# Two plain pairs instead of three before Strassen's algorithm in the output projection, and PSUM banks dealt round-robin over three tiles

## The chip, the cores and the metric

The kernel runs on one core of a Trainium2 chip. The metric is the device time of one execution in microseconds (us); the median of the runs counts.

## What is computed

Four sequences of 448 tokens pass through a talking-heads attention with 12 heads of 64 columns. The result, 1792 tokens by 768 columns, is the input `x` of this layer:

```python
h = x @ w_in                                  # 1792 x 1024
sm = softmax(h); solu = h * sm
ln = (solu - mean) / sqrt(var + 1e-6) * g_ln
out = ln @ w_out                              # 1792 x 768, float32
```

The change concerns only the last product, `ln @ w_out`, with 1024 rows and 768 columns in `w_out`.

## The kernel before, in words

Tokens go in 14 tiles of 128 (`NT = 14`). Each tile's 1024 hidden columns are made by 36 matmuls of 512 columns (`hidden`, L984) in one of three PSUM tiles `h_banks` of two banks each, `h_banks[t % 3]`. VectorE, ScalarE and GpSimd turn them into the SoLU and the layer norm (L1559 to L1659), as a high and a low fp16 half, `lh` and `ll`. Both halves are stored to DRAM (`zS`, L1662) and read back transposed into `lt` by a DMA on SyncE's queue (`zT`, `turn`, L1674).

The output projection handles tiles in seven pairs (`NPP = 7`). Each operand is split in a high and a low half, and each product sums three terms (high by high, high by low, low by high), all matmuls with 384 output columns (`project`, L1751). The first `NPL` pairs are **plain**: four products (two tiles by two halves of the columns), each over all eight blocks of 128 rows of `w_out`, so 24 matmuls each and 96 for the pair. They go in turn to the PSUM tiles of `ps_x` and `ps_y`, one bank each. The other pairs go by **Strassen's algorithm** (in Winograd's form) over the 2 by 2 blocks of the pair of tiles and `w_out`: seven products of 12 matmuls, 84 for the pair. For these a pair needs a **front**: two sums of the halves of `lt` into `xs` (`pair_whole`, L1689), four sums of blocks (`pair_sum`, L1702), two casts on ScalarE (`part_hi`, L1707) and two differences (`part_lo`, recorded at L1511). The emission of a Strassen product (`emit`) is one copy on ScalarE (product 0, L1772) or one or two VectorE operations (L1783), nine in all; that of a plain product is one scaled copy on either engine (L1762, L1764).

`w_out` too needs sums of its blocks, made in place from `wo_raw`, block row by block row k = 0 to 3: scaling (`zs`, L1506), four subtractions on VectorE (`zt`, L1511, into `tt` and `wo`), casts on ScalarE (L1541) and differences on VectorE (`zL`, L1511). The last of them overwrites the right half of the upper half of `wo_h` and `wo_l`, and so follows the first two products of the last plain pair (`zP`, `NPL - 1`).

The order of the work on each engine comes from a planner, `moe.order()`: it simulates the engines, takes for each the task that can start first, and among tasks that can start within 0.143 us the one with the earliest due time. The engines then run their instructions in that order, each waiting for what it needs. The due times of the projection follow `T = TP + TQ * (7 * i + min(i, NPL))`, 1.94 us per 12 matmuls: a pair's front is due 18 to 12 us before the pair, its emissions 12 us before the end of their product, so long overdue when they can run. The sums of `w_out` are due at fixed times (120 + 4 k).

Memory also hangs on `NPL`. `lt` of a pair lies in one of two `lt` buffers, except for the pairs `NPL` and `NPL + 1`, which take over `xf1` and `xf2`, the buffers of the inputs of batches 1 and 2. `xs` of pair `NPL` takes over `xf0`; the later ones take turns in the two `raw` buffers, which are free once `wo_raw` has been used up:

```python
n = i - NPL + 1
if 0 < n < B - 1:
    x = wt_p.tile(x_in[n].shape, F16, tag=f"xf{n}", name=f"lt_{i}")
```

The six Strassen banks are the two banks of each of the three tiles `h_banks`; `bank(i, j)` says which product takes which. The planner counts six banks (`B=6`). The semaphores come from the tile framework.

Of the kernel before, what the change touches and what calls it, by code (L numbers as in the profile page):

```python
# [240 lines left out]
def kernel(  # L241
# [82 lines left out]
    def spread_steps(out, am, n, name, bank):  # L324


        ps = []

        def turn():
            ps.append(bank(f"spread_{name}"))  # L330
            for i in range(n):
                nc.tensor.matmul(
                    ps[0][:, i * 128 : (i + 1) * 128],
                    am[:, i : i + 1].to_broadcast([128, 128]),
                    ident32,
                    start=True,
                    stop=True,
                )

        def take():  # L340
            x = ps[0][:, 0 : n * 128].rearrange("p (n f) -> p n f", n=n)
            nc.vector.tensor_reduce(out=out, in_=x, axis=AX.X, op=ALU.max)

        return [("pe", turn), ("dve", take)]

    def scale_steps(am, n, e, name, bank, pool=const):

        t = pool.tile([128, 2], F32, name=f"amx_{name}")
        own, am1 = t[:, 0:1], t[:, 1:2]
        s, inv, steps = pow2_steps(am1, 1, e, name, pool)  # L350

        def join():
            nc.vector.tensor_reduce(out=own, in_=am, axis=AX.X, op=ALU.max, apply_absolute_value=True)

        steps = [("dve", f) for f in steps]
        return s, inv, [("dve", join)] + spread_steps(am1, own, 1, name, bank) + steps
# [600 lines left out]
    NT = NTOK // 128  # L957
# [3 lines left out]
    h_banks, hps = [], {}  # L961
# [439 lines left out]
    with tc.manual_schedule():  # L1401
# [91 lines left out]
            nc.vector.tensor_scalar(out=c_out, in0=i_o, scalar1=2.0**-E_LN, scalar2=None, op0=ALU.mult)  # L1493

        KH, DH, FH = KFF // 2, DM // 2, DFF // 2
        NPP, NPL = NT // 2, 3
        STEPS = [(i, j) for i in range(NPP) for j in range(4 if i < NPL else 7)]
        tz, tts = {}, {}

# [232 lines left out]

        def bank(i, j):
            n = (7 * (i - NPL) + j) % 6
            return h_banks[n // 2][:, n % 2, 0:DH]

        def project(i, j):
            if i < NPL:
# [334 lines left out]
```

## Time and profile before

| | us |
|---|---|
| median of 3 runs (646.65 to 649.11) | 648.18 |
| the profiled execution itself | 645.8 |
| its span, first to last instruction | 644.1 |
| TensorE busy in the span | 619.3 |
| VectorE busy in the span | 542.9 |

The profiled execution takes 1.7 us beyond its span, and lies 2.4 us under the median of the runs. In the rows below times are from the start of the span. A row of the timeline says when it begins, how long it lasts, engine, line, operation, out<-in, and in square brackets the idle time of the engine before it with what ended it. PE is TensorE, DVE VectorE, ACT ScalarE, POOL GpSimd, SPq and ACTq the queues of SyncE and ScalarE.

### The profile page before, as it was taken

To read this page: it belongs to the slowest core of one execution; us is meant where nothing else is said; L and a number is where in the kernel's file an instruction comes from. 1 tells how busy PE (TensorE), PEld (TensorE's weight loads), DVE (VectorE), ACT (ScalarE), POOL (GpSimd) and SP (SyncE) were. 2 spreads that over 40 slices of the span, in tenths; PEclk is the share of its full clock that TensorE was granted. 3 is DMA by queue.
4 is the path that set the end of the run, shared out by engine and by line. 5 is a ranking of instruction groups with operands and counts; after the bars stand their busy time and mean duration, and the time that the engine had idled before them with its cause. 6 is when DMAs were issued, how large, how long until landed. Compare 5 with 4: busy or idle time off the path is not lost.

```text
span 644.1 us, 17785 instructions
## 1 busy us (share of the span) xinstructions
PE 619.3 (96%) x6612; PEld 425.6 (66%) x6612; DVE 542.9 (84%) x1361; ACT 471.3 (73%) x1046; POOL 280.3 (44%) x427
## 2 busy tenths in 40 slices
PE   7889989999999999999999999999999999999995
PEld 7557767777767778777877777774444445566663
DVE  7879997789988689996999989848999698877873
ACT  5788978999888898988989997726766688432120
POOL 2125773255844254594354246403688656400000
PEclk9999999999999999999999999999999999999998
DMA  9057488466678448779746763019993111896122
GB/s 257 3 194 233 152 171 179 156 201 211 207 170 181 149 137 241 239 167 235 239 145 229 218 209 122 3 35 340 263 270 83 67 65 50 202 213 142 50 82 66
DMA packets 118063, 105.88 MB, mean 164 GB/s; under 512 B 70052, under 2 KB 105176, under 8 KB 117976
## 3 DMA queue, kind: packets, MB, share of 16 engines
q1 hardware_dynamic: 110456, 86.88, 47.6%
q0 software_dynamic: 4416, 12.40, 7.1%
q10 hardware_dynamic: 3104, 5.46, 2.7%
q8 instruction: 52, 0.85, 0.6%
q14 instruction: 35, 0.29, 0.1%
HBM read 33.24 MB, written 16.97 MB: 78 GB/s over the span
## 4 chain that ended last, share of the span: by engine, by line
PE 62%; DVE 19%; ACT 7%; issue 4%; POOL 3%; DMA 3%; SPq 1%; DVEq 0%; ACTq 0%; POOLq 0%
PE po L766 15%; PE ps_h L984 13%; PE ps_h L1751 8%; PE px L815 7%; PE pm L711 6%; PE ps L644 6%; PE y L1751 5%; DVE dead L721 4%; DVE s L661 3%; ACT e L737 3%; DMA sr<-s 2%; ACT s L656 2%; DVE hl_k L365 2%; POOL wr L758 1%; DVE wo_l L365 1%
## 5 line engine op out<-in xcount | busy, mean ns | idle before, releaser
L766 PE MATMUL po<-wr,e 128*112 128x120 f32 x1440 | 175.0, 272 | 6.4 <-POOL wr L758 4.9
L766 PEld LDWEIGHTS po<-wr,e 128*112 128x112 f32 x1440 | 155.7, 177 | 36.6 <-POOL wr L758 15.9
L758 POOL TENSOR_SCALAR wr<-wq,sm 128x120 f32<-128x120 f32 x180 | 77.3, 437 | 180.5 <-DVE sm L752 93.4
L737 ACT ACTIVATE e<-pm,nb,c_exp 128x448 f32<-128x448 f32 x180 | 131.5, 735 | 18.6 <-DVE dead L721 9.4
L721 DVE TENSOR_SCALAR_CACHE_REDUCE dead<-pm,c_nexp 128x448 f16<-128x448 f32 x180 | 121.7, 676 | 11.5 <-PE pm L711 7.5
L661 DVE SCALAR_TENSOR_TENSOR s<-ps,s 120x448 f16<-120x448 f32 (+1 forms) x192 | 112.2, 615 | 14.4 <-ACT s L656 13.9
L369 ACT COPY p_t<-po 112x480 f32<-112x480 f32 x180 | 108.2, 625 | 11.1 <-PE po L766 9.8
L656 ACT ACTIVATE s<-ps 120x448 f16<-120x448 f32 (+1 forms) x192 | 97.5, 554 | 16.4 <-PE ps L644 15.8
L815 PE MATMUL px<-p_t,raw_v 112*64 112x120 f32 (+3 forms) x1632 | 86.8, 259 | 0.8 <-ACT e L737 0.7
L815 PEld LDWEIGHTS px<-p_t,raw_v 112*64 112x64 f32 x1632 | 76.1, 137 | 16.1 <-issue 11.0
L984 PE MATMUL ps_h<-wi,xf 128*128 128x512 f16 x396 | 85.8, 379 | 0.0
L644 PE MATMUL ps<-k,q 64*64 64x448 f16 (+2 forms) x1008 | 78.5, 354 | 3.1 <-DVE s L661 2.3
L984 PEld LDWEIGHTS <-xf 128*128 128x128 f16 x396 | 38.7, 98 | 46.5
L1751 PEld LDWEIGHTS <-lt 128*128 128x128 f16 x432 | 42.3, 98 | 28.9 <-issue 1.0
L711 PE MATMUL pm<-sr,wp_hi 64*64 64x448 f16 x720 | 56.4, 359 | 2.1 <-DMA sr<-s 1.1
L644 PEld LDWEIGHTS <-q 64*64 64x64 f16 (+2 forms) x1008 | 34.5, 106 | 24.6 <-issue 8.3
L1751 PE MATMUL y<-wo_h,lt 128*128 128x384 f16 x192 | 47.2, 326 | 0.6 <-DVE o L1764 0.6
L1659 POOL TENSOR_TENSOR ll<-u,lh 128x1024 f16<-128x1024 f32 x14 | 33.3, 2379 | 11.4 <-ACT lh L1655 11.4
L737 ACT ACTIVATION_READ_ACCUMULATOR e<-pm,nb,c_exp 128x1 f32 x180 | 37.8, 210 | 0.0
L711 PE MATMUL pm<-sr,wp_lo 64*64 64x448 f16 (+1 forms) x360 | 36.1, 349 | 0.0
L365 DVE SCALAR_TENSOR_TENSOR xsl<-px,x_sc,xsh 128x120 f16<-128x120 f32 (+1 forms) x96 | 25.9, 325 | 7.9 <-ACT xsh L360 7.9
L748 DVE TENSOR_SCALAR sm<-sm 128x2 f32<-128x2 f32 (+1 forms) x92 | 18.8, 204 | 15.1 <-ACT e L737 14.4
(209 smaller groups left out, 950.4 us busy)
## 6 DMA issues: line engine op xcount, KB each, us to landing
sr<-s SPq DMA_DIRECT2D x176, 210.0 KB
cv_wi<-in_moe_w_in_dram SPq DMA_DIRECT2D x24, 256.0 KB
cv_wo<-in_moe_w_out_dram SPq DMA_DIRECT2D x8, 768.0 KB
raw_k<-in_k_dram POOLq DMA_DIRECT2D x18, 224.0 KB, 3.6
raw_q<-in_q_dram POOLq DMA_DIRECT2D x18, 224.0 KB, 5.0
raw_v<-in_v_dram POOLq DMA_DIRECT2D x18, 224.0 KB, 3.9
ln_h<-lh SPq DMA_DIRECT2D x14, 256.0 KB
ln_l<-ll SPq DMA_DIRECT2D x14, 256.0 KB
```

The source lines that it names most:

```text
L369: nc.scalar.copy(out=out, in_=in_)
L644: nc.tensor.matmul(sps[b, c, h + e][lo:hi], q2[b, g][rows, 2 * j + x, i0 + lo : i0 + hi], k1[b, g][rows, 2 * j + y], start=(a == 0), stop= ...
L656: nc.scalar.activation(out=s_t[b, c][0 : y.shape[0], h, 0], in_=y, func=AF.Copy, scale=2.0**-E_S)
L661: nc.vector.scalar_tensor_tensor(out=t[:, h, 1], in0=y, scalar=2.0**-E_S, in1=t[:, h, 0], op0=ALU.mult, op1=ALU.subtract)
L711: nc.tensor.matmul(pmx[b, u + i][64 * e : 64 * e + 64, 0:S], w[rows], sr[b, u][rows, e, z], start=(a == 0), stop=(a == 2),)
L721: nc.vector.tensor_scalar(out=dead, in0=pmx[b, u][:, 0:S], scalar1=c_nexp[0:UK, b : b + 1], scalar2=None, op0=ALU.mult, op1=ALU.min, accum ...
L737: nc.scalar.activation(out=ee[b, u], in_=pmx.pop((b, u))[:, 0:S], func=AF.Exp, bias=nbs.pop((b, u)), scale=c_exp[0:UK, b : b + 1], accum_o ...
L758: ENG[eng].tensor_scalar(out=w, in0=wq[0:UK, 0 : H * UN], scalar1=sm, scalar2=1.0, op0=ALU.mult, op1=ALU.mult)
L766: nc.tensor.matmul(ps[:, c * 120 : (c + 1) * 120], e[:, c * CP : (c + 1) * CP], w, start=True, stop=True)
L815: nc.tensor.matmul(xps[b, blk, g][e * 64 : e * 64 + 64, i, cut], raws["v", b, p][:, e, c * D : (c + 1) * D], next(x for y, x in block_view ...
L984: nc.tensor.matmul(ps[:, n], xx[:, kc, o : o + 128], ww[:, kc, n * 512 : (n + 1) * 512], start=(kc == 0 and a == 0), stop=(kc == KDM - 1 a ...
L1751: nc.tensor.matmul(y, x, w, start=(n == 0), stop=(n == len(terms) - 1 ))
```

## The change

Two plain pairs are left of three, so that pairs 2 to 6 go by Strassen's algorithm. Product n (counted through all Strassen pairs) takes bank n div 3 of tile n mod 3 in place of bank n mod 2 of tile n div 2 (n taken mod 6).

```diff
         KH, DH, FH = KFF // 2, DM // 2, DFF // 2
-        NPP, NPL = NT // 2, 3
+        NPP, NPL = NT // 2, 2
         STEPS = [(i, j) for i in range(NPP) for j in range(4 if i < NPL else 7)]
         tz, tts = {}, {}
...
         def bank(i, j):
             n = (7 * (i - NPL) + j) % 6
-            return h_banks[n // 2][:, n % 2, 0:DH]
+            return h_banks[n % 3][:, n // 3, 0:DH]
```

## Rows read from the trace of the kernel before

**Rows 1.** The page: busy us of the engines, share of the span, instructions.
```profile
PE 619.3 (96%) x6612; PEld 425.6 (66%) x6612; DVE 542.9 (84%) x1361; ACT 471.3 (73%) x1046; POOL 280.3 (44%) x427
```
**Rows 2.** Chain that ended last, by time: start, us, engine, tile, line, count.
```profile
432.30 79.17 PE ps_h L984 x366
...
551.18 31.45 PE y L1751 x192
582.63 54.61 PE ps_h L1751 x336
```
**Rows 3.** Windows, whole projection: us, then busy (count) PE, PEld, DVE, ACT, POOL, PEclk, DMA.
```profile
534.84:637.30 102.46, 101.81 (x625) 60.95 (x623) 77.62 (x113) 33.93 (x57) 16.04 (x10) 1.00 0.52 121
```
**Rows 4.** Waits of TensorE, 430 to 644 us: total, times, longest.
```profile
PE y L1751 <- DVE o L1764: 0.6, 1, 0.6
```
**Rows 5.** Groups of instructions, 540 to 644.1 us: busy, mean ns, idle before.
```profile
L1702 DVE TENSOR_TENSOR xs<-xs 128x512 f32<-128x512 f32 x16 | 11.0, 688 | 0.4
...
L1511 DVE TENSOR_TENSOR sz<-xs,sz 128x1024 f16<-128x1024 f32 x8 | 9.7, 1217 | 0.4 <-ACT sz L1707 0.4
L1783 DVE SCALAR_TENSOR_TENSOR o<-ps_h,c_out,xs 128x384 f32<-128x384 f32 x16 | 9.6, 612 | 4.6 <-PE ps_h L1751 4.6
L1689 DVE TENSOR_TENSOR xs<-lt 128x1024 f32<-128x1024 f16 x8 | 9.6, 1218 | 0.0
```
**Rows 6.** Timeline of the first Strassen pair, at the boundaries of its products.
```profile
584.41 0.33 PE L1751 MATMUL ps_h<-tz_h,lt 128*128 128x384 f16 x1
...
586.37 0.33 PE L1751 MATMUL ps_h<-wo_h,lt 128*128 128x384 f16 x1
...
586.57 0.58 ACT L1772 ACTIVATE xs<-ps_h,c_out 128x384 f32<-128x384 f32 x1 [3.32 <-PE ps_h L1751]
...
590.47 0.62 DVE L1783 SCALAR_TENSOR_TENSOR o<-ps_h,c_out,xs 128x384 f32<-128x384 f32 x1 [0.93 <-PE ps_h L1751]
...
597.22 0.61 DVE L1783 SCALAR_TENSOR_TENSOR o<-ps_h,c_out,xs 128x384 f32<-128x384 f32 x1
```
**Rows 7.** Timeline of VectorE at the end, after the last matmul.
```profile
637.27 0.62 DVE L1783 SCALAR_TENSOR_TENSOR o<-ps_h,c_out,o 128x384 f32<-128x384 f32 x1 [1.58 <-PE ps_h L1751]
637.80 1.13 DVE L1783 SCALAR_TENSOR_TENSOR o<-ps_h,c_out,xs 128x384 f32<-128x384 f32 x2
```
**Rows 8.** Windows, two stretches of stores (columns as in rows 3; last is GB/s).
```profile
630.50:632.60 2.10, 2.10 (x15) 1.26 (x14) 0.18 (x1) 0.00 (x0) 0.00 (x0) 1.00 0.33 94
638.90:642.20 3.30, 0.00 (x0) 0.00 (x0) 0.04 (x1) 0.00 (x0) 0.00 (x0) 0.74 0.69 178
```
**Rows 9.** Windows, before and in the plain pairs (columns as in rows 3).
```profile
505.00:512.00 7.00, 7.00 (x35) 3.38 (x34) 2.71 (x10) 4.50 (x10) 2.89 (x3) 1.00 0.29 112
512.00:527.00 15.00, 15.00 (x71) 6.82 (x70) 14.33 (x26) 12.42 (x20) 8.01 (x5) 1.00 0.14 53
527.00:543.00 16.00, 16.00 (x89) 8.43 (x87) 13.04 (x30) 13.13 (x29) 7.10 (x7) 1.00 0.13 51
543.00:551.00 8.00, 7.60 (x47) 4.47 (x46) 7.86 (x7) 4.34 (x8) 7.51 (x5) 1.00 0.30 118
551.00:567.00 16.00, 15.82 (x97) 9.48 (x97) 12.91 (x20) 8.88 (x14) 4.19 (x2) 1.00 0.97 212
```
**Rows 10.** Timeline of VectorE: sums of w_out, an emission, w_out's last difference.
```profile
545.43 2.30 DVE L1511 TENSOR_TENSOR tt<-wo,tt 128x384 f32<-128x384 f32 x1
547.77 2.36 DVE L1511 TENSOR_TENSOR wo<-wo,tt 128x384 f32<-128x384 f32 x1
550.05 0.55 DVE L1511 TENSOR_TENSOR wo<-wo,wo 128x384 f32<-128x384 f32 x1
550.52 0.60 DVE L1764 TENSOR_SCALAR o<-y,c_out 128x384 f32<-128x384 f32 x1
...
565.23 0.55 DVE L1511 TENSOR_TENSOR tz_l<-wo,tz_h 128x384 f16<-128x384 f32 x1
```
**Rows 11.** Windows, the second Strassen pair (columns as in rows 3).
```profile
596.10:609.80 13.70, 13.70 (x87) 8.25 (x85) 11.75 (x17) 2.67 (x3) 0.00 (x0) 1.00 0.21 59
```

## The prediction

> **What bounds the kernel now.** I read the page first: TensorE is busy for 619.3 of 644.1 us of the span [rows 1]. The chain that ended last shows where this binds. From 432.3 us on it names long runs of TensorE, and its last two, 31.45 and 54.61 us, are the projection up to 637.24 us [rows 2]; what lies between the runs is work behind TensorE, since the windows show it busy for 101.81 of 102.46 us of the projection at the full granted clock, 2.4 GHz [rows 3]. Third, its waits: one, of 0.6 us, for a VectorE emission [rows 4]. So in this stage a matmul saved is time saved, until VectorE comes too late. After the last matmul 6.9 us of the span are left (644.1 - 637.24). The sum is made against the profiled execution's own 645.8 us (span 644.1 and 1.7 around it) and carried to the median, 648.18 us, 2.4 us above it.
>
> **Matmuls removed.** Pair 2 needs 84 matmuls in place of 96. 336 take 54.61 us, 0.1625 us each [rows 2], so 12 x 0.1625 = **-1.95 us**, all on the path. Bounds: 12 x 0.164 from the plain run (31.45 / 192) and 12 x 0.1625: one answer.
>
> **Banks.** An emission is late in a regular way. Product 0 of the first Strassen pair ends near 584.4, where product 1 begins; its emission waits until 586.57, just after product 1 ended at 586.4 [rows 6]. Product 2 ends at 588.3, its emission starts at 590.47, at the end of product 3 [rows 6]. Both times the two products share a PSUM tile, in different banks: the wait is for the tile. Afterwards the next product lies in another tile, and an emission can begin as its own product ends. In mid-stage this gains nothing, as TensorE doesn't wait. At the end it does. The last pair has product 5 in the first bank of a tile and product 6 in its second, so product 5's two operations run only after product 6, at 637.27 and the first half of 637.80, ahead of product 6's own, which ends at 638.93 [rows 7]. Afterwards product 5 is emitted during product 6, and product 6's one operation runs at 637.27 and ends at 637.89: **-1.04 us**. The stores follow. Now a whole tile and half of one, 178 GB/s x 3.3 us = 587 KB, go out together and end near 642.1, 3.2 us after the last emission; half a tile alone, 94 x 2.1 = 197 KB, was out 1.9 us after its emission ended at 630.7 [rows 8]. Afterwards the whole tile's emission ends 1.13 us behind product 5 (637.24 - 1.95 + 1.13 = 636.4), 1.5 us ahead of the half's: up to **-1.3 us** more. Bounds -1.04 (the stores still collide) and -2.34 (they don't); I take **-2.0**, nearer the second, since 393 KB at 178 GB/s need 2.2 us and overlap the half's store for 0.7 us only.
>
> **The front of one more pair.** 2 x 1.218 + 4 x 0.688 + 2 x 1.217 = **7.6 us of VectorE** [rows 5], and two casts on ScalarE, which is busy 8.88 of 16 us there [rows 9] and covers them. Emissions: nine operations of 0.61 [rows 5] and one on ScalarE in place of four, some 3 us more, but late, where VectorE has 1.95 us free in a pair's 13.7 us with a front included [rows 11]. The 7.6 us come early: the Strassen pairs now begin 96 matmuls, 15.6 us, sooner, at about 567 us, and front 2 must be done 3 products later. Its due time lies ahead of those of w_out's sums, so the planner puts it before them. Its input is no obstacle: `lt` of pair 2 moves into `xf1`, free when the last tile of batch 1 has been multiplied, four hidden tiles of 36 x 0.2163 = 7.8 us before 534.84, so at 503.7 [rows 2, 3]. These four transposes move from behind plain pair 0 to there, on SyncE's queue ahead of layer-norm stores; what those feed is transposed 20 us later or more, so I cost it at nothing (uncovered it would be 4 issues).
>
> Where does front 2 fit? VectorE is idle for 4.29 us from 505 to 512, of which at most half comes after the transposes have landed; for 0.67 to 527, 2.96 to 543, and 0.14 to 551 [rows 9]: at best 5.9 us. The rest, and idle time that sits inside dependent chains, pushes the queue. Behind it on VectorE stand the sums of w_out and, in order, the emission of plain pair 0's third product. Before, that emission ran at 550.52 and already held TensorE for the 0.6 us of rows 4; all matmuls of pair 1 queue behind it. Why it is late shows above it: two of w_out's subtractions of 384 columns took 2.30 and 2.36 us, the next 0.55 [rows 10], while GpSimd was busy 7.51 of 8 us [rows 9]. The Trainium skill (page "SBUF — State Buffer", section "Who interferes with whom") says that a VectorE instruction with two SBUF inputs and a GpSimd instruction that reads SBUF exclude each other for a whole instruction. The trace agrees with that, and the rule speaks against this change, whose eight new VectorE operations all have two SBUF inputs and fall beside the layer norm.
>
> The cost has no row of its own. From below: -0.6 us, if the planner's new order puts the emission earlier. From above: 7.6 us of work and half of the eight operations stretched by 1.8 us (2.36 - 0.55), 14.8 us, less 5.9 of idle time: 8.9 us. I take **+2.1 us** of new stall at plain pair 1: 7.6 less the 3.8 us idle from 512 to 551 leaves 3.8, and of w_out's sums ahead of the emission (4 x 0.55 = 2.2) some will be planned behind it. It is nearer to the lower end because TensorE, once held, gives every later user that much slack: the stalls do not add, the largest counts.
>
> **Later.** w_out's last difference ended at 565.8 us [rows 10], with 3.1 us of VectorE idle in the last 16 [rows 9]; their use begins after about 568.7, so a delay of 3 us is covered, the more so after the stall. Front 3 can start only when `wo_raw` is free, near 571, and is needed at about 586: 7.6 us and seven products' emissions, 5.5, fit into 15.
>
> **The new wait.** If a tile is the unit, product n+3 now waits for emission n (before: n+6 for n and n+1). From the end of product n to the start of n+3 there are two products, 3.9 us. Product 5 of the first pair ended at 584.41 + 5 x 1.95 = 594.2 and its emission at 597.83 [rows 6]: 3.6 us, with two of the old waits before it. I cost it at nothing; if the cover goes, some tenths each time, and everything on TensorE queues behind.
>
> **Sum.** -1.95 - 2.0 + 2.1 = -1.85 us: from 645.8 to 643.95 for the profiled execution, **646.3 us** for the median.
>
> **Rivals.**
> First: no new stall. For it: planned early, front 2 has up to 5.9 us of gaps, and w_out's sums may be planned behind the emission. Against: rows 4 and 10 show the emission late already. Time 648.18 - 3.95 = 644.2; 643.6 if the old 0.6 goes too.
> Second, slower: VectorE is the bound at plain pair 1. Every second operation of front 2 is held by GpSimd, the stall is 8.9 us, the time 648.18 - 3.95 + 8.9 = 653.1. For it: rows 10; against: of 39 us before 551 only the last 8 have GpSimd at 94%, the others at about half [rows 9]. The time is above that of before from 4.0 us of stall. By the page's rule just cited this is what must happen if the front is planned into those last 8 us.
> Third: product n+3 waits for emission n. At 0.7 us once in each of five pairs, 3.5 us, without the forecast's stall: 647.7. For: 3.6 of 3.9 us used. Against: that lateness is mostly the wait that the change takes away.
> Fourth, the change does not do what it says: the emissions wait for something other than the tile, the tail stays, and with my stall 648.3 comes out. Rows 6 and 7 speak against it.
>
> **Chances.** Forecast 0.40, first 0.32, second 0.12, third 0.10, fourth 0.06. About 0.5%, 3.2 us, can be told from no change here. Faster by more (under 644.9): the first and a little of the forecast, 0.34. Slower by more (over 651.4): most of the second, 0.10. Same: 0.56. The range takes in the first with the old stall gone and the tail's lower bound (648.18 - 1.95 - 2.34 - 0.6 = 643.3), the third and fourth, and the second up to half of its stall beyond the forecast's: 643.0 to 650.5.
>
> **What would show it.** Right: 612 matmuls in the projection; the first emission of a pair begins at the end of its own product; after the last matmul one VectorE operation, and 4.6 to 5.9 us of span left; TensorE's waits with one of 2 to 3.5 us for the emission of plain pair 0, behind two-input operations at 1.4 us or more. Wrong: no such wait (then the first), waits for Strassen emissions in each pair (third), several us of waits for `tz` or `sz` (front or sums late), or a tail of 6.9 us.

## The result: 7.6 us faster, more than the range allowed

The changed kernel took a median of 640.68 us (639.51 to 641.25, 5 runs) against 648.26 us (646.65 to 649.11, 5 runs) of the kernel before in the same comparison: ratio 0.9896, interval 0.9866 to 0.9926. The forecast was 646.3 us, with a range of 643.0 to 650.5. The same kernel compared again (below) gave 0.9936 (0.9914 to 0.9958). A ratio of 0.992 lies in both intervals, and it is what the profiles show: the output projection with its tail (the time from the last matmul to the end of the span) is **5.1 us** shorter.

### The profile page after: what moved, and what is told of

Its sections match the earlier page's. It is cut to its first block, busy times and chain, and to the rows that moved or that the text cites. A ratio compares the mean times of both kernels' runs of the same rounds, so it can differ in the third digit from the quotient of the medians.

```text
span 637.8 us, 17788 instructions
## 1 busy us (share of the span) xinstructions
PE 617.1 (97%) x6600; PEld 424.3 (67%) x6600; DVE 552.5 (87%) x1378; ACT 473.2 (74%) x1045; POOL 285.0 (45%) x427
## 3 DMA queue, kind: packets, MB, share of 16 engines
q10 hardware_dynamic: 2720, 4.42, 2.3%
## 4 chain that ended last, share of the span: by engine, by line
PE 69%; DVE 14%; ACT 7%; issue 3%; POOL 3%; DMA 2%; SPq 0%; DVEq 0%; ACTq 0%; POOLq 0%
PE ps_h L984 17%; PE po L766 15%; PE ps_h L1751 11%; PE px L815 8%; PE ps L644 6%; PE pm L711 6%; PE y L1751 5%; DVE dead L721 3%; DVE s L661 3%; ACT e L737 3%; ACT s L656 2%; DVE hl_k L365 2%; POOL wr L758 1%; DMA raw_q<-in_q_dram 1%; ACT p_t L369 1%
## 5 line engine op out<-in xcount | busy, mean ns | idle before, releaser
L656 ACT ACTIVATE s<-ps 120x448 f16<-120x448 f32 (+1 forms) x192 | 97.6, 555 | 16.2 <-PE ps L644 15.6
L1751 PEld LDWEIGHTS <-lt 128*128 128x128 f16 x372 | 36.4, 98 | 24.2
L1659 POOL TENSOR_TENSOR ll<-u,lh 128x1024 f16<-128x1024 f32 x14 | 31.9, 2276 | 11.4 <-ACT lh L1655 11.2
L1751 PEld LDWEIGHTS <-sz 128*128 128x128 f16 x240 | 23.5, 98 | 15.5
```

What stands on the lines that cost most here:

```text
L656: nc.scalar.activation(out=s_t[b, c][0 : y.shape[0], h, 0], in_=y, func=AF.Copy, scale=2.0**-E_S)
L1751: nc.tensor.matmul(y, x, w, start=(n == 0), stop=(n == len(terms) - 1 ))
```

## The profile after

The profiled execution took 639.51 us, its span is 637.8. First the page's busy times, against [rows 1]:

```profile
PE 617.1 (97%) x6600; PEld 424.3 (67%) x6600; DVE 552.5 (87%) x1378; ACT 473.2 (74%) x1045; POOL 285.0 (45%) x427
```

TensorE works 2.2 us less and VectorE 9.6 us more. The chain that ended last, against [rows 2]:

```profile
431.04 79.17 PE ps_h L984 x366
...
510.43 23.38 PE ps_h L984 x108
533.81 31.20 PE y L1751 x192
565.01 68.26 PE ps_h L1751 x420
```

From 431 us up to the last matmul the chain is TensorE alone, and the list of TensorE's waits is empty from 420 us to the end: the 0.6 us of [rows 4] are gone. 612 matmuls end at 633.27, and the span ends 4.53 us later, where it was 6.86. The windows, against [rows 3] and [rows 9]:

```profile
512.00:527.00 15.00, 15.00 (x71) 6.75 (x70) 14.90 (x24) 13.39 (x22) 7.13 (x5) 1.00 0.10 37
527.00:543.00 16.00, 16.00 (x90) 8.66 (x89) 15.64 (x29) 14.33 (x27) 11.70 (x8) 1.00 0.63 119
543.00:551.00 8.00, 8.00 (x51) 4.81 (x50) 7.90 (x13) 6.38 (x13) 3.99 (x3) 1.00 0.44 159
551.00:567.00 16.00, 16.00 (x101) 9.63 (x99) 15.59 (x25) 8.34 (x15) 5.80 (x4) 1.00 0.79 180
567.00:583.00 16.00, 16.00 (x100) 9.65 (x99) 15.76 (x23) 3.26 (x4) 0.00 (x0) 1.00 0.58 134
533.81:633.30 99.49, 99.45 (x613) 59.69 (x610) 87.19 (x131) 34.36 (x54) 18.75 (x11) 1.00 0.49 114
```

The fourth number is VectorE's. From 512 to 583 us it is idle for 1.2 us in 71: the front of the additional pair has filled every gap, and still TensorE (the second number) waits for nothing. Where the emission that was expected to be late stands, shows VectorE's timeline:

```profile
542.57 2.46 DVE L1511 TENSOR_TENSOR tt<-wo,tt 128x384 f32<-128x384 f32 x1
...
545.98 1.28 DVE L1587 SCALAR_TENSOR_TENSOR u<-ps_h,sm,u 128x1024 f32<-128x1024 f32 x1
...
547.18 0.61 DVE L1764 TENSOR_SCALAR o<-y,c_out 128x384 f32<-128x384 f32 x1
...
549.52 0.55 DVE L1511 TENSOR_TENSOR tt<-wo 128x384 f32<-128x384 f32 x1
550.11 2.37 DVE L1511 TENSOR_TENSOR tt<-wo,tt 128x384 f32<-128x384 f32 x1
```

L1764 is the emission of plain pair 0's third product. It begins at 547.18, at 550.52 before [rows 10], although more work lies before it in all: the sums of `w_out`'s block row 1 (from 549.52 on) now come behind it. The end, against [rows 7]:

```profile
631.35 0.62 DVE L1783 SCALAR_TENSOR_TENSOR o<-ps_h,c_out,o 128x384 f32<-128x384 f32 x1 [0.68 <-PE ps_h L1751]
...
632.52 1.74 SPq L2035 DMA_DIRECT2D out_dram<-o  x2
632.52 1.80 ACTq L2035 DMA_DIRECT2D out_dram<-o  x2
...
633.30 0.62 DVE L1783 SCALAR_TENSOR_TENSOR o<-ps_h,c_out,xs 128x384 f32<-128x384 f32 x1 [0.81 <-PE ps_h L1751]
```

Product 5 ends at 633.27 - 1.95 = 631.32 and is emitted at once; its stores leave at 632.52, and only one operation is left after the last matmul.

## The experiments

The question is what the gain is made of and why no stall came. Medians scatter by some us, but one stretch hardly does, so every profile was read in the same way: the **projection** runs from the first matmul of L1751 in the timeline to the end of the last one in the chain, the **tail** from there to the end of the span.

| kernel | projection | tail | sum | ratio to before (interval) |
|---|---|---|---|---|
| before | 102.40 | 6.86 | 109.26 | |
| before, again | 102.40 | 6.85 | 109.25 | 0.9999 (0.9981 to 1.0016) |
| emission first | 101.57 | 6.92 | 108.49 | 0.9991 (0.9971 to 1.0010) |
| banks alone | 102.38 | 4.45 | 106.83 | 0.9977 (0.9955 to 0.9998) |
| pairs alone | 99.61 | 6.01 | 105.62 | 0.9950 (0.9927 to 0.9972) |
| the change | 99.62 | 4.53 | 104.15 | 0.9896 (0.9866 to 0.9926) |
| the change, again | 99.62 | 4.41 | 104.03 | 0.9936 (0.9914 to 0.9958) |
| sums first | 101.26 | 4.46 | 105.72 | 0.9941 (0.9917 to 0.9965) |
| front twice | 99.62 | 4.44 | 104.06 | 0.9963 (0.9940 to 0.9986) |
| late sum | 102.92 | 4.42 | 107.34 | 0.9957 (0.9936 to 0.9978) |
| two PSUM tiles | 99.69 | 4.43 | 104.12 | 0.9916 (0.9889 to 0.9942) |
| late store | 99.63 | 4.65 | 104.28 | 0.9954 (0.9921 to 0.9986) |
| store behind | 99.62 | 5.84 | 105.46 | 0.9924 (0.9898 to 0.9950) |
| one plain pair | 113.30 | 4.50 | 117.80 | 1.0136 (1.0107 to 1.0165) |

("Pairs alone": there the chain does not pass through the last product, so the end is taken from the timeline, whose last matmul begins at 633.66 and takes 0.33 us: 633.99.)

### Both kernels once more, no edit

> The kernel before, unchanged, against itself. Both theories: ratio 1.000, within 0.2%. It gives the scatter: theory one (the stage before the projection only scatters) expects the projection to begin anywhere from 533.5 to 536 us in profiles of one and the same kernel; theory two (the change also makes the attention faster, by 1 to 2 us) expects 534.8 within 0.3 us, as in the profile before.

> The change as it is. Theory one: 5.3 us of the difference lie in the projection and its tail (1.95 matmuls, 1.0 stalls of TensorE, 2.3 behind the last matmul), the rest is scatter, so the difference comes out nearer to 5.3 than to 7.6 us and the projection begins at a scattered time. Theory two: 7 us or more again, and the projection begins 1 us or more sooner than in the null run.

The kernel before repeats itself: 0.9999, and its projection begins at 535.05 us, which fits both theories. The change is again faster, but by 4.5 us in the medians (642.57 against 647.06), not 7.6, and its projection begins later, at 541.97: theory one. Its profiled run took 647.76 us, though projection and tail are as short as in the first. The time is lost before, which the chain shows:

```profile
306.72 6.30 DMA cv_wi<-in_moe_w_in_dram
...
313.04 10.89 DMA cv_wi<-in_moe_w_in_dram
...
438.37 71.41 PE ps_h L984 x330
...
511.14 3.21 DMA lt<-ln_l
...
514.42 3.13 DVE xs L1689
...
524.48 3.08 DVE xs L1689
...
532.86 1.30 DVE u L1587 x2
534.20 7.93 PE ps_h L984 x36
```

Two things. The long run of hidden matmuls begins at 438.37, at 431.04 in the first profile, after loads of `w_in` that don't stand in the first chain; up to there the order of TensorE's instructions is the same in both kernels. In 14 profiles it begins between 431.04 and 438.37, so that the attention alone scatters by 7 us, and the first profile is the earliest of all. And the run now breaks off after 330 matmuls: the last hidden tile waited 0.9 us, and the chain leads back over both L1689 operations of the new front to the transposes. That wait comes with the change, and the forecast had it nowhere (why it is 0 in one profile and 0.9 in the other: last section).

### One half of the change at a time

```diff
-        NPP, NPL = NT // 2, 3
+        NPP, NPL = NT // 2, 2
```

> Two plain pairs, banks as before. Theory that the banks give the tail: 12 matmuls (1.95 us) and the old stall go (1.0 us), the tail behind the last matmul stays at 6.9 us: 3 us faster than before. Rival: with one more Strassen pair the products are counted from another start, the last pair's product 5 takes bank 33 mod 6 = 3 (second of the middle tile) and product 6 bank 34 mod 6 = 4 (first of the last tile), so they lie in different tiles with the old dealing too: the tail is 4.5 us and the whole gain of 5.3 us is there without the new banks.

```diff
-            return h_banks[n // 2][:, n % 2, 0:DH]
+            return h_banks[n % 3][:, n // 3, 0:DH]
```

> Three plain pairs, banks dealt over the tiles. Theory: 624 matmuls, the stall of 0.6 us at the second plain pair stays, emissions of the first product of a pair begin at the end of their own product, the tail goes from 6.9 to 4.5 us: 2.3 us faster than before, and TensorE waits for no Strassen emission. Rival (product n+3 waits for emission n too often): waits of TensorE for VectorE or ScalarE in each Strassen pair, 2 to 4 us in all, and no gain.

The banks alone give -2.43 us, all in the tail, and leave the 0.6 us wait as it was. The pairs alone take 2.79 us off the projection: 1.95 of matmuls and 0.8 for the wait, which is gone. They also give 0.85 of the tail, which is between the theory (nothing) and the rival (all of it), since counting from pair 2 puts the last two products into different tiles:

```profile
632.08 0.62 DVE L1783 SCALAR_TENSOR_TENSOR o<-ps_h,c_out,xs 128x384 f32<-128x384 f32 x1 [2.10 <-PE ps_h L1751]
...
633.79 1.13 DVE L1783 SCALAR_TENSOR_TENSOR o<-ps_h,c_out,xs 128x384 f32<-128x384 f32 x2
```

Here product 4 waits for its mate 5 (until 632.08), so four operations of products 4 and 5 stand ahead of product 6's, which ends at 634.92, 0.93 us after the last matmul. So the halves overlap by about 1 us: -2.43 - 3.64 would be -6.1, and the whole gives -5.1.

### Why the old stall went: the planner's order

On the kernel before, the sums of block row 1 were put behind the emission; on the changed kernel, the emission behind these sums.

```diff
 # emission first, on the kernel before: the task zt of w_out's sums
+                    behind=[("zE", 0, 2)] if (k, i) == (1, 0) else [],
 # sums first, on the changed kernel: the task zE
-                behind=[("zE",) + x for x in before],
+                behind=[("zE",) + x for x in before] + ([("zt", 1, 3)] if (i, j) == (0, 2) else []),
```

> The kernel before, but the planner must put the sums of w_out's block row 1 behind plain pair 0's third emission. Theory (the order alone made the old stall): TensorE's wait of 0.6 us goes and the projection and its tail take 108.3 us in place of 109.3. Rival (the old stall came from GpSimd slowing VectorE, whatever the order): the wait stays at 0.5 us or more.

> The change, but the planner must put plain pair 0's third emission behind the four sums of w_out's block row 1, as it stood in the kernel before. Theory (the forecast stall was right in its mechanism and did not come because the planner put the emission ahead of these sums): the emission, at 547.2 us in the changed kernel, now follows operations that end there at 554 us, so TensorE waits 3 to 5 us at the second plain pair and the projection and its tail take 107 to 109 us in place of 104.0. Rival (VectorE has slack there whatever the order): a wait under 1 us, 104 to 105 us.

The order is enough to remove the stall. With the emission first the kernel before has no wait, and its projection is 0.83 us shorter, at 101.57; the change then has exactly 101.57 - 1.95 = 99.62. (In the kernel before the sums ahead of the emission were also stretched [rows 10]; no run takes the stretch away and leaves the order, so what each is worth alone stays open.) The run with the sums first did not reach its order on the engines: the planner put the emission later, but gave it to ScalarE, where it ran behind ScalarE's own work and before the last of these sums on VectorE:

```profile
551.91 0.56 ACT L1762 ACTIVATE o<-y,c_out 128x384 f32<-128x384 f32 x1
...
552.52 0.32 PE L1751 MATMUL y<-wo_h,lt 128*128 128x384 f16 x1 [1.48 <-ACT o L1762]
...
553.87 0.55 DVE L1511 TENSOR_TENSOR wo<-wo,wo 128x384 f32<-128x384 f32 x1
```

So it shows that a late place of this emission costs the changed kernel too, 1.64 us here, against the rival. The 3 to 5 us expected behind the sums on VectorE were not measured. An estimate from this trace is 3.9: the next emission of a plain product on VectorE, L1764 right behind the sums, ends at 554.95, and TensorE was free from 552.52 - 1.48 = 551.04.

### Where the front of one more pair costs

The two L1689 operations of pair 2 were done twice; in another kernel the second of them was put behind the SoLU work of tile 10.

```diff
 # front twice
+            for _ in range(2 if i == NPL else 1):
                 ENG[eng].tensor_tensor(
 # late sum
+                    behind=[("zp", 10)] if i == NPL and t else [],
```

> The change, with each of the two first sums of pair 2's front done twice (two more VectorE operations of 128x1024, 2.4 us, unknown to the planner). Theory (VectorE has no slack left between 505 and 527 us: the SoLU product that the last hidden tile needs ended 0.2 us before that tile): the last hidden tile begins 2 to 4 us late, the plain pairs show no wait, and the whole is 2 to 4 us slower than the change. Rival (there is slack of some us): no new wait of TensorE, no difference.

> The change, but the second of the two first sums of pair 2's front is planned behind the SoLU product that the last hidden tile needs. Theory: that product comes 2 to 3 us sooner than in the change, the last hidden tile never waits (it waited 0.9 us in one profile of the change, 0 in the other), the front still ends before it is needed and the projection stays at 104.0 us: 0 to 0.9 us faster than the change, 5 to 6 us faster than before. Rival (the front pushed back meets the plain pairs' emissions): waits of TensorE of 1 us or more at the second plain pair or at pair 2.

With twice the front the projection is untouched (99.62), and the whole price stands at the last hidden tile, whose PSUM tile is free only when VectorE's L1587 has read it. First the waits of TensorE in this kernel, then in the one with the late sum:

```profile
PE ps_h L984 <- DVE u L1587: 2.3, 1, 2.3
```

```profile
PE y L1751 <- DVE o L1764: 2.8, 3, 1.3
```

The late sum frees the hidden tile and pays 3.3 us in the projection, in three waits for plain emissions. The rival holds. Of the two places tried the planner's, ahead of the last hidden tile, is the better one, at 0 to 0.9 us; other places were not tried.

### The new wait of product n + 3

```diff
-            n = (7 * (i - NPL) + j) % 6
-            return h_banks[n % 3][:, n // 3, 0:DH]
+            n = (7 * (i - NPL) + j) % 4
+            return h_banks[n % 2][:, n // 2, 0:DH]
```

(with the planner's count at B=4)

> The changed kernel with Strassen's products dealt over the four banks of two tiles instead of the six of three, so that product n+2 waits for the emission of product n (now n+3). It measures how near the added wait was to deciding. A product has 12 matmuls of 0.1625 us = 1.95 us; emission n has that long after product n's end, where the three tiles gave 3.9 us. In the changed kernel's steady pairs an emission ends 1.3 to 3.6 us after its product. Theory (the wait on the emission of n is met with 3.9 us but would not be with 1.95): TensorE shows waits on VectorE or ScalarE in most of the five pairs, 0.5 to 1.7 us each, and projection to end of span grows from 104.0 to 107 to 116 us. Rival (the emissions keep up because nothing forces them late; their late ends are only queueing behind work with no due time): 104.0 to 105.

The rival holds: with 1.95 us in place of 3.9 no wait comes, and projection and tail stay at 104.12. Why shows the changed kernel's own timeline, at the first product of the second and the third Strassen pair:

```profile
580.71 0.58 ACT L1772 ACTIVATE xs<-ps_h,c_out 128x384 f32<-128x384 f32 x1 [4.43 <-PE ps_h L1751]
...
594.36 0.58 ACT L1772 ACTIVATE xs<-ps_h,c_out 128x384 f32<-128x384 f32 x1 [5.04 <-PE ps_h L1751]
```

These products end 96 and 180 matmuls after 565.01, at 580.6 and 594.3 (0.1625 us each); the emission begins 0.1 us later. The expectation put the emissions' ends at 1.3 to 3.6 us behind their products; in the second pair the timeline has 0.7 to 1.6. The first pair is later. Its product 0 is emitted 1.4 us after its end, at 568.41, released by `w_out`'s last difference, and product 5, which ended at 576.71, is done 1.9 us later, against the 3.6 us of [rows 6]:

```profile
577.96 0.61 DVE L1783 SCALAR_TENSOR_TENSOR o<-ps_h,c_out,xs 128x384 f32<-128x384 f32 x1
```

So about half of the 3.6 us were old waits for the mate. With two PSUM tiles the latest emission of the first pair ends 1.8 us after its product, just inside the 1.95.

### The stores in the tail

Two kernels were to hold tile b's store back. The first issued it after product 6, the second also fixed its queue behind tile a's store.

```diff
 # both
-                goes = {2: [(a, 0, 1)] if last else [], 5: [(b, 0, 2)], 6: [(a, int(last), 2)]}.get(j, [])
+                goes = {2: [(a, 0, 1)] if last else [], 5: [] if last else [(b, 0, 2)], 6: [(a, int(last), 2)] + ([(b, 0, 2)] if last else [])}.get(j, [])
 # store behind
-                        {"sp": 0.6, "act": 0.6},
+                        {("sp", "act")[x]: 0.6} if (i, j) == (NPP - 1, 6) else {"sp": 0.6, "act": 0.6},
+                        behind=[("zO", a, x)] if (i, j, t) == (NPP - 1, 6, b) else [],
```

> The changed kernel with one edit: in the last pair the store of the whole tile b goes out only after product 6, behind the two stores of tile a's half, instead of after product 5. Theory (a tail of 4.5 us against 6.9 came from two things: one emission instead of two after the last matmul, and tile b's store landing before tile a's last half is issued): from the last matmul to the end of the span grows from 4.5 to 5.5 to 5.9 us, and first matmul of the projection to end of span from 104.0 to 105.0 to 105.3. Rival (the stores share 16 DMA engines and the last bytes need the same time either way; the whole gain was the emission): 104.0 stays within 0.3. The median alone, with a scatter of some us in the attention ahead, will hardly tell the two apart.

> The changed kernel with the last pair's stores put in a forced order on their queues: on SyncE's and on ScalarE's queue the store of tile a's second half stands first, and tile b's whole store behind it, so that b's 393 KB can't leave before product 6 is emitted. (In the run with the late store this wasn't reached: each queue got the stores of one tile, and b's left at the end of product 5's emission all the same.) Theory (the change's tail fell by 2.3 us for two reasons, 1.04 us of emission and 1.25 us because tile b's store leaves one product earlier): from the last matmul to the end of the span grows from 4.5 to 5.4 to 5.9 us, and from the projection's first matmul to the end of the span from 104.1 to 105.0 to 105.5. Rival (the last bytes need the same time in either order, and the tail went only by the emission and by chance): 4.4 to 4.7, and 104.0 to 104.3. Either way the median says little, as the attention ahead scatters by some us.

The first did not hold the store back and says nothing on the theory. In its timeline SyncE's queue took tile b's stores alone, and they left at the end of product 5's second operation (633.06 + 0.61), although the plan had them later:

```profile
633.06 0.61 DVE L1783 SCALAR_TENSOR_TENSOR o<-ps_h,c_out,xs 128x384 f32<-128x384 f32 x1
...
633.70 1.17 SPq L2035 DMA_DIRECT2D out_dram<-o  x2
...
635.12 0.82 ACTq L2035 DMA_DIRECT2D out_dram<-o  x2
```

The second held it back, and the tail is 640.9 - 635.06 = 5.84 us in place of 4.53: +1.3, as the theory had it. The tail's gain is 1.04 of emission and 1.3 of a store that leaves earlier.

### One plain pair instead of two

```diff
-        NPP, NPL = NT // 2, 2
+        NPP, NPL = NT // 2, 1
```

> The changed kernel with one plain tile pair less ahead of the first Strassen pair (NPL 2 to 1: that would be six pairs by Strassen's algorithm and one plain tile pair the fewer). Theory (each pair moved to Strassen takes 12 matmuls = 1.95 us off TensorE and moves the need for all sums of w_out 15.6 us forward; the sums of w_out end at 568 in the changed kernel and its first Strassen product begins at 565, so that sums needed from 549.4 on come up to 15 us late): TensorE waits for VectorE's sums at the first Strassen pair, 8 to 17 us in all, and projection to end of span is 109 to 119 us, against 104.0; slower than the kernel before. Rival (VectorE orders its work by due time and has room ahead of the projection, so the sums move forward and only the 7.6 us front of one more pair is new): 102 to 105 us.

Here VectorE is the bound, as the forecast's second rival had it for the change itself. Its waits of TensorE, and windows around them:

```profile
PE ps_h L1751 <- ACT tz_h L1541: 8.8, 3, 4.3
PE ps_h L1751 <- DVE tz_l L1511: 3.2, 3, 1.7
```

```profile
550.00:555.00 5.00, 5.00 (x33) 3.03 (x31) 4.93 (x11) 4.96 (x11) 2.03 (x2) 1.00 1.04 258
555.00:560.00 5.00, 1.73 (x11) 0.82 (x9) 5.00 (x9) 2.98 (x7) 2.22 (x2) 1.00 1.03 243
560.00:565.00 5.00, 0.67 (x3) 0.16 (x2) 4.60 (x7) 3.95 (x7) 2.08 (x2) 0.63 0.85 162
565.00:570.00 5.00, 1.26 (x4) 0.36 (x3) 4.93 (x7) 1.66 (x3) 1.35 (x1) 0.50 0.27 105
570.00:575.00 5.00, 4.36 (x15) 2.07 (x14) 4.56 (x7) 0.00 (x0) 0.00 (x0) 0.50 0.00 0
575.00:580.00 5.00, 5.00 (x33) 2.99 (x32) 4.44 (x8) 2.04 (x2) 0.00 (x0) 1.00 0.02 3
```

The projection is 113.30 us where 99.62 - 1.95 = 97.67 would have been: 15.6 us lost, 12.0 of them waits for casts and differences of `w_out`'s sums, and part of the rest a lower clock (last section). The kernel is 1.4% slower than before. VectorE is busy for 4.56 to 5.00 us of every 5 there. Two plain pairs cover those sums, one does not.

## Why the prediction was wrong

**Right.** *Matmuls removed*: -1.95 us, exactly (101.57 to 99.62). *Banks*: an emission waited for its tile mate and no longer does. *Tail*: taken at -2.0, it measured -2.33 and in the repeat -2.45; the stores don't collide, so the outer bound, -2.34, was the value, and 0.3 us of the miss are here. *Later*: the sums of `w_out` ended at 567.74 + 0.55 and no wait followed. *The new wait*, costed at nothing: nothing, and the first pair's product 5 now uses 1.9 of the 3.9 us.

**The step that failed** is "I take +2.1 us of new stall at plain pair 1". It kept the order of before, with most of the sums of `w_out` ahead of the emission (only a share of their 2.2 us was to go behind it), and pushed that queue back by the front. The planner orders anew: with the front's work in the list, block row 1's sums came behind the emission. The stall wasn't new, and the old one of 0.6 us went (0.8 in the projection). That is 2.9 us between forecast and fact. The prediction named this order, as a lower bound and as its first rival's condition, and gave its time, 643.6. By the projection and tail alone it would be 648.18 - 5.1 = 643.1 us, just inside the range. The rest of the way to 640.68 lies ahead of the projection, and the repeat (642.57) shows less of it.

**A cost in the wrong place.** The front does take VectorE's time, but the bill comes 15 us sooner, at the last hidden tile. The text asked "where does front 2 fit?" and counted gaps; it didn't ask which chain runs through the stretch from 505 to 527, where L1587 of the last tiles frees a PSUM tile for TensorE. Before, L1587 ended 2.5 us ahead (524.5, while the last tile began 36 x 0.2163 before 534.84, at 527.05); now it ends 0.2 us ahead (525.82 against 533.81 - 7.79) or 0.9 us too late. The change has used up this slack; which of the two it is hangs on how late VectorE runs already (last section).

**What is left** of the 7.6 us, some 2.5, lies ahead of the projection. The repeat (-4.5 us) and the scatter of the attention speak for scatter and against a part of the change. As one execution per kernel is profiled, it can't be shown run by run. In projection and tail no kernel that was run is shorter than the change (104.0 to 104.2).

## What to carry to other kernels

When a planner orders the work, an added task isn't a block that pushes a fixed queue: forecast the order first, and bound a stall by both orders. To find what added work costs, look at each deadline that its engine serves in that stretch (here the PSUM tile of the last hidden tile), not only at the wait that already shows. And where the median scatters more than the effect, read the stretch that the change touches: here it repeats within 0.1 us.

## What was not expected of the hardware

**A VectorE operation that begins beside one of GpSimd ends a fixed time behind it.** GpSimd's L1659 and VectorE's L1689 in the changed kernel, first run, then the repeat:

```profile
506.02 2.13 POOL L1659 TENSOR_TENSOR ll<-u,lh 128x1024 f16<-128x1024 f32 x1 [1.43 <-ACT lh L1655]
...
507.07 2.16 DVE L1689 TENSOR_TENSOR xs<-lt 128x1024 f32<-128x1024 f16 x1 [2.06 <-DMA lt<-ln_l]
...
515.80 2.35 POOL L1659 TENSOR_TENSOR ll<-u,lh 128x1024 f16<-128x1024 f32 x1 [1.37 <-ACT lh L1655]
...
516.08 3.15 DVE L1689 TENSOR_TENSOR xs<-lt 128x1024 f32<-128x1024 f16 x1
```

```profile
514.34 2.12 POOL L1659 TENSOR_TENSOR ll<-u,lh 128x1024 f16<-128x1024 f32 x1 [1.42 <-ACT lh L1655]
...
514.42 3.13 DVE L1689 TENSOR_TENSOR xs<-lt 128x1024 f32<-128x1024 f16 x1 [1.08 <-DMA lt<-ln_l]
```

In all three VectorE's operation, begun 0.1 to 1.1 us after GpSimd's, ends 1.1 us after it (509.23 against 508.15, 519.23 against 518.15, 517.55 against 516.46), whatever its start; alone it takes 1.22 [rows 5]. This is what the Trainium skill (page "SBUF — State Buffer", section "Who interferes with whom") states, an exclusive lock, and the trace agrees. In "pairs alone" VectorE began first, by 0.07 us, and GpSimd's operation took 3.14 us in place of 2.13:

```profile
507.69 1.23 DVE L1689 TENSOR_TENSOR xs<-lt 128x1024 f32<-128x1024 f16 x1 [0.94 <-DMA lt<-ln_l]
507.76 3.14 POOL L1659 TENSOR_TENSOR ll<-u,lh 128x1024 f16<-128x1024 f32 x1 [1.43 <-ACT lh L1655]
```

The 3.13 against 2.16 us do not make the 0.9 us at the last hidden tile. The transposes landed equally late in both profiles, 76.0 us after the long run of hidden matmuls began; GpSimd and VectorE were 1.0 us later against TensorE in the repeat, and were so at the last L1587 ahead of the front (72.2 us after that begin, against 71.2). L1689 ends behind GpSimd's operation either way, so the lag stays. VectorE fell behind in the fourth hidden tile, where it waited for a load of `w_out`:

```profile
467.52 2.01 DVE L898 TENSOR_SCALAR cv_wo<-cv_wo 128x768 uint32<-128x768 uint32 x1 [0.64 <-DMA cv_wo<-in_moe_w_out_dram]
```

This wait is not the change's: "emission first" and "banks alone" have it too, without the additional front. With the front it goes along with the wait at the last hidden tile: "store behind" (0.8 us) and "one plain pair" (1.0) show both, the first profile, "late store", "sums first" and "two PSUM tiles" neither. Only "pairs alone" has the first without the second: there VectorE went ahead of GpSimd.

**After a long stall TensorE also ran slower.** With one plain pair TensorE was busy for 1.73 and 0.67 of 5 us, and the granted clock fell to 0.63 and then 0.50, 1.2 GHz. Back at work, at 1.2 GHz it did 15 matmuls in 4.36 us (570 to 575), at 2.4 GHz then 33 in 5.00.
